# Quadrant tables for batches 0 and 1, and a new order, engines and banks for the opening of an attention and feed-forward kernel

## The chip, the cores and the metric

The kernel runs on one core of a Trainium2 chip. The metric is device time in microseconds (us). Three runs of the kernel before gave 321.02, 321.51 and 321.62 us, so its median is 321.51 us.

## What is computed

Eight batches of sliding-window attention with ALiBi slopes (8 heads, 576 tokens, 64 per head), and on its output a feed-forward layer with a hard swish. All inputs and the output are float32.

```python
def _attn_ref(q, k, v):                      # 8 x 8 x 576 x 64
    scores = scale * np.matmul(q, k.transpose(0, 1, 3, 2))
    slopes = 2.0 ** (-8.0 * (np.arange(H) + 1) / H)
    bias = slopes[:, None, None] * (-np.abs(rel))[None, :, :]   # rel = query - key
    mask = (rel >= 0) & (rel < 128)
    attn = softmax(np.where(mask, scores + bias[None], -1e9))
    return np.matmul(attn, v)
def _moe_ref(x, w_in, w_out):                # x 4608 x 512, w_in 512 x 2048
    h = x @ w_in
    return (h * np.clip(h + 3.0, 0.0, 6.0) / 6.0) @ w_out
```

## The kernel before, in words

**Attention.** A group g is one pair of heads of one batch: 8 batches of 4 pairs make 32 groups, g = 4 * batch + pair. A group's q and k are transposed to 64 x 576 for each head. Since the window is 128, each of the five key tiles of 128 needs two blocks of scores: the diagonal block, and the block with the next query tile. Both are made transposed (keys on partitions) in one of two score areas of PSUM, each of two banks, which take turns (`score_banks`). ScalarE takes the exponential into bf16 weights, `av_matmuls` multiplies them with v (with a column of ones, whose product is the sum), VectorE divides (`attend`, `attend_split`, `values`), and the result is transposed into xT (`back`), where the feed-forward layer reads it.

**Masks and slopes.** Where a group is *tabled*, a table of slope * (key - query), with -2^30 outside the window, is first written into the PSUM area by matmuls with the identity as weights, and the scores are added on top; the exponential then takes 1024 columns at once. In batch 0 both halves are tabled (`tables_diag`, `tables_off`), in batch 1 only the off half. Everything else takes slope and position through the exponential's bias, head by head, and GpSimd sets what is masked to zero (`affine_select`).

**Feed-forward.** xT's 4608 tokens are cut into 9 blocks of 512. A *unit* is four matmuls with 512 columns each: an up unit (`moe_up`, 16 for a block; ScalarE's relu and VectorE's product follow) or a quarter of a down product (`moe_down`, 16 for a block). A string, ORDER, gives the order of U and D; `fill(n)` runs the next n units, and FILLS gives the counts at seven places of each group.

**Order.** The program is scheduled by hand: every engine runs its instructions in the order of the code, and waits on semaphores. `first_batch` and `second_batch` write out the opening, groups 0 to 7 (batches 0 and 1, all tabled in part); `segment` then runs groups 8 to 31 with their fills. Transfers are issued from the queues of SP (q, k, v, the first quarter of w_in as float32), ScalarE (the first k) and GpSimd (the other weights, cast on the way). Where weights are not loaded yet, their room is used: batch 0's exponentials lie in w_out_sb, batch 1's in gbuf 1. Line numbers are those of the kernel before: L163 warm-up matmuls, L238 and L269/L281/L301 transposes of q and k, L321 and L357/L360 tables, L346 and L372/L378 scores of the opening, L399 scores after it, L422/L409 exponentials, L144 tables' making, L484/L485 division, L517 transposes of the result, L532 up and L587 down matmuls.

Of the kernel before, what the change touches and what calls it, by code (L numbers as in the profile page):

```python
# [18 lines left out]
def kernel(  # L19
# [29 lines left out]
    NB_FULL = 2  # L49
# [9 lines left out]
    tab = perm.tile([128, H, 2, 128], BF16)  # L59
# [20 lines left out]
    p4buf = [held.tile([128, 2, 128], BF16, name=f"p4buf{i}") for i in range(2)]  # L80
# [42 lines left out]

    def constants():
# [5 lines left out]
        base = rpool.tile([128, NT], FP32, tag="r6", name="base")  # L130
        base_i = base[:, 0:256].bitcast(INT32).rearrange("p (s c) -> p s c", s=2)
        base_b = base[:, 256:384].bitcast(BF16).rearrange("p (s c) -> p s c", s=2)
        nc.gpsimd.iota(base_i, pattern=[[128, 2], [0, 128]], base=-192, channel_multiplier=1)
        nc.gpsimd.tensor_copy(out=base_b, in_=base_i)
        biases()
        nc.gpsimd.affine_select(out=base_b[:, 1, :], in_=base_b[:, 1, :], pattern=[[1, 128]],
                                channel_multiplier=-1, base=0,
                                compare_op=ALU.is_ge, fill=-(2.0 ** 30))
        nc.gpsimd.affine_select(out=base_b[:, 0, :], in_=base_b[:, 0, :], pattern=[[-1, 128]],
                                channel_multiplier=1, base=-1,  # L140
                                compare_op=ALU.is_ge, fill=-(2.0 ** 30))
        nc.vector.memset(kTb[0][:, :, 4, LAST:128], 0.0)
        for h in range(H):
            nc.vector.tensor_scalar(out=tab[:, h, :, :], in0=base_b, scalar1=slopes[h] / scale,  # L144
                                    scalar2=0.0, op0=ALU.mult, op1=ALU.add)

    def memsets():
        nc.gpsimd.memset(vbuf[0][:, :, :, D:W], 1.0)
        nc.gpsimd.memset(vbuf[0][64:128, 4, :, 0:D], 0.0)

    def memsets_later():
        for i in range(2):
            nc.gpsimd.memset(p4buf[i], 1.0)
        nc.gpsimd.memset(kTb[1][:, :, 4, LAST:128], 0.0)
        nc.gpsimd.memset(vbuf[1][:, :, :, D:W], 1.0)
        nc.gpsimd.memset(vbuf[1][64:128, 4, :, 0:D], 0.0)
        nc.gpsimd.memset(tbuf[64:128, :, 4, :], 0.0)
# [7 lines left out]
    def biases():  # L165
        nc.vector.tensor_copy(out=rel_f, in_=rel_i)
        for h in range(H):
            nc.vector.tensor_scalar(out=bias_o[:, h:h + 1], in0=rel_f, scalar1=-192.0,
                                    scalar2=slopes[h], op0=ALU.add, op1=ALU.mult)

        for h in range(H):
            nc.vector.tensor_scalar(out=bias_d[:, h:h + 1], in0=rel_f, scalar1=-64.0,
                                    scalar2=slopes[h], op0=ALU.add, op1=ALU.mult)
# [20 lines left out]
    def second_w_in():  # L194
        nc.gpsimd.memset(w_out_sb[:, 4, 0:1], 0.0)
        load_w_in(1)
# [24 lines left out]
    st = {}  # L221

    def prepare(g, copies):
        for nm, copy in zip("qk", copies):
            pr = prs.tile([128, RT * D], BF16, tag=f"pr{nm}", name="pr",
                          padded_shape=[128, 2 * RT * D])
            copy(out=pr, in_=runs[nm][:, g % NP, :])
            st[g, nm] = pr

    def transposes(g, copies):  # L230
        b, hp = divmod(g, NP)
        for nm, dst, copy in (("q", qTb[b % 2], copies[0]), ("k", kTb[b % 2], copies[1])):
            src = st.pop((g, nm))
            tp = ps_h.tile([128, RT, RP], BF16, tag="h", name="tp", padded_shape=[128, 16, 64])
            for t in range(RT):
# [74 lines left out]
    def full(g):  # L310
        return g < NB_FULL * NP

# [574 lines left out]
```

## Time and profile before

| | us |
|---|---|
| median of three runs | 321.51 |
| the profiled execution: span from its first to its last instruction | 317.9 |
| TensorE busy in it | 307.0 |
| ScalarE busy | 196.8 |
| VectorE busy | 176.1 |
| GpSimd busy | 138.9 |
| opening: start of group 8's scores (L399) | 49.66 |
| start of group 9's scores | 59.97 |
| start of group 14's scores | 96.04 |

In the profile PE is TensorE, PEld its weight loads, DVE VectorE, ACT ScalarE, POOL GpSimd, SP the engine that only issues transfers. A row of the timeline has the start in us, the time taken, engine, line, operation, output and inputs, shapes, and how many instructions are merged; in brackets the idle time of the engine before it and what ended it. Matmuls overlap one another in the array, so the time between two starts says more than a duration.

### The profile page before, as it was taken

The numbers are of one execution on the slowest core, as the hardware profiler recorded it, in microseconds if no ns is written. First come the engines' busy times: TensorE is split into PE (matmuls) and PEld (weight loads), VectorE is DVE, ScalarE is ACT, GpSimd is POOL, SyncE is SP. The second block draws the span as 40 slices with busy tenths as digits, with TensorE's granted clock in tenths as the row PEclk, the third lists the DMA queues.
The fourth block names the chain that finished last, engine by engine and source line by source line (L and its number), as shares of the span: only waits on it lengthen the run. The fifth ranks groups of instructions, "written<-read, shape, count | busy, mean of one in ns | idle before, by whom it ended". The sixth has DMA issues, their size and how long they took to land.

```text
span 317.9 us, 6980 instructions
## 1 busy us (share of the span) xinstructions
PE 307.0 (97%) x2671; PEld 163.4 (51%) x2710; DVE 176.1 (55%) x344; ACT 196.8 (62%) x338; POOL 138.9 (44%) x247
## 2 busy tenths in 40 slices
PE   8889999999999999999999999999999999999996
PEld 3565474455554445555676644454444444444443
DVE  6677676554456654566465546564656455455510
ACT  3869986877767666766667756675764244244401
POOL 7358192674594684548463854472231000000000
PEclk9999999999999999999999999999999999999999
DMA  7999999999999999999999999934112100000112
GB/s 271 264 373 215 255 236 200 236 235 198 216 265 180 222 215 212 213 196 253 186 178 219 190 206 198 228 95 57 49 29 75 66 34 33 35 33 33 66 57 77
DMA packets 131425, 52.43 MB, mean 165 GB/s; under 512 B 118976, under 2 KB 122816, under 8 KB 131392
## 3 DMA queue, kind: packets, MB, share of 16 engines
q1 hardware_dynamic: 125648, 46.15, 69.0%
q0 software_dynamic: 3696, 3.67, 7.1%
q10 hardware_dynamic: 2048, 2.16, 2.2%
q8 instruction: 21, 0.34, 0.5%
q14 instruction: 12, 0.10, 0.1%
HBM read 36.70 MB, written 9.44 MB: 145 GB/s over the span
## 4 chain that ended last, share of the span: by engine, by line
PE 90%; ACT 3%; DVE 3%; issue 2%; POOL 0%; DVEq 0%; POOLq 0%; ACTq 0%
PE hps L532 38%; PE ops L587 37%; PE score L399 3%; PE av L463 2%; PE av L455 2%; DVE avs L485 1%; PE ops L568 1%; PE w L163 1%; ACT w_out_sb L422 1%; PE score L346 1%; PE tp L269 1%; ACT r L556 1%; DVE gbuf L557 1%; PE score L301 1%; PE score L357 1%
## 5 line engine op out<-in xcount | busy, mean ns | idle before, releaser
L556 ACT ACTIVATE r<-hps,bias 128x512 f32<-128x512 f32 x144 | 98.9, 689 | 84.2 <-PE hps L532 83.9
L557 DVE SCALAR_TENSOR_TENSOR gbuf<-r,hps 128x512 bf16<-128x512 f32 x144 | 98.8, 688 | 91.6 <-ACT r L556 90.1
L532 PE MATMUL hps<-xT,w_in_sb 128*128 128x512 bf16 (+1 forms) x623 | 142.0, 358 | 1.7 <-ACT xT L519 0.3
L587 PE MATMUL ops<-w_out_sb,gbuf 128*128 128x512 bf16 x538 | 133.8, 379 | 2.3 <-issue 1.8
L532 PEld LDWEIGHTS <-w_in_sb 128*128 128x128 bf16 x640 | 59.2, 98 | 54.0 <-issue 1.5
L587 PEld LDWEIGHTS <-gbuf 128*128 128x128 bf16 x560 | 52.4, 98 | 57.5
L427 POOL TENSOR_SCALAR_AFFINE_SELECT pd<-pd 128x512 bf16<-128x512 bf16 x48 | 29.4, 631 | 35.2 <-ACT pd L425 35.2
L436 POOL TENSOR_SCALAR_AFFINE_SELECT po<-po 128x512 bf16<-128x512 bf16 x48 | 30.1, 633 | 30.8 <-ACT po L434 30.1
L596 DVE COPY osb<-ops 128x512 f32<-128x512 f32 x33 | 22.7, 688 | 23.8 <-PE ops L587 23.7
L425 ACT ACTIVATE pd<-score,bias_d 128x512 bf16<-128x512 f32 x48 | 31.1, 683 | 6.4 <-PE score L399 6.4
L434 ACT ACTIVATE po<-score,bias_o 128x512 bf16<-128x512 f32 x48 | 33.1, 690 | 0.0
L213 POOL CAST tbuf<-ldbuf 128x512 bf16<-128x512 f32 (+1 forms) x45 | 25.7, 611 | 15.7 <-issue 14.6
L474 DVE TENSOR_TENSOR avs<-av,rc 128x384 bf16<-128x384 f32 (+1 forms) x48 | 23.6, 491 | 1.6
L463 PEld LDWEIGHTS <-pd 128*128 128x128 bf16 x192 | 14.3, 97 | 8.2 <-issue 0.2
L455 PE MATMUL av<-vbuf,po 128*128 128x65 bf16 x192 | 18.0, 193 | 0.0
L206 POOL CAST vbuf<-ldbuf 128x1024 bf16<-128x1024 f32 x14 | 14.3, 1041 | 7.6 <-DMA ldbuf<-in_v_dram 7.6
L463 PE MATMUL av<-vbuf,pd 128*128 128x65 bf16 x192 | 17.3, 194 | 0.0
L455 PEld LDWEIGHTS <-po 128*128 128x128 bf16 x192 | 14.3, 98 | 3.0 <-DVE avs L474 0.5
L439 ACT ACTIVATE p4buf<-score,bias_d 128x64 bf16<-128x64 f32 x48 | 15.6, 324 | 0.0
L399 PEld LDWEIGHTS <-kTb 64*64 64x64 bf16 x480 | 9.4, 106 | 9.1 <-issue 8.5
L399 PE MATMUL score<-qTb,kTb 64*64 64x192 bf16 (+1 forms) x480 | 13.1, 234 | 0.0
L246 POOL CAST pr<-ldbuf 128x576 bf16<-128x576 f32 x18 | 11.5, 668 | 2.6 <-PE tp L238 1.3
(107 smaller groups left out, 201.7 us busy)
## 6 DMA issues: line engine op xcount, KB each, us to landing
out_dram<-osb SPq DMA_DIRECT2D x33, 256.0 KB, 3.5
ldbuf<-in_v_dram SPq DMA_DIRECT2D x31, 256.0 KB, 4.6
ldbuf<-in_q_dram SPq DMA_DIRECT2D x20, 256.0 KB, 5.0
ldbuf<-in_k_dram SPq DMA_DIRECT2D x16, 256.0 KB, 5.3
ldbuf<-in_q_dram SPq DMA_DIRECT2D x12, 288.0 KB, 6.6
ldbuf<-in_k_dram SPq DMA_DIRECT2D x12, 288.0 KB, 6.7
w_out_sb<-in_moe_w_out_dram POOLq DMA_DIRECT2D x4, 512.0 KB, 9.1
w_in_sb<-in_moe_w_in_dram POOLq DMA_DIRECT2D x3, 512.0 KB, 8.8
```

Source lines behind the costliest of these rows:

```text
L213: nc.gpsimd.tensor_copy(out=tbuf[:m, :, j, :], in_=s[:m, j, :, :].rearrange("p (i e) d -> p i (e d)", e=2))
L399: nc.tensor.matmul(wide[e][c, ds(at, n)], lhsT=kT[r, j, c], rhs=qT[r, ds(q0, n)], start=True, stop=True)
L425: nc.scalar.activation(out=pd[:, e, :, :], in_=block_scores(g, e, False), func=ACT.Exp, bias=bias_d[:, h:h + 1], scale=scale)
L427: nc.gpsimd.affine_select(out=pd[:, e, :, :], in_=pd[:, e, :, :], pattern=[[0, 4], [1, 128]], channel_multiplier=-1, base=0, compare_op=AL ...
L434: nc.scalar.activation(out=po[:, e, :, :], in_=sc, func=ACT.Exp, bias=bias_o[:, h:h + 1], scale=scale)
L436: nc.gpsimd.affine_select(out=po[:, e, :, :], in_=po[:, e, :, :], pattern=[[0, 4], [-1, 128]], channel_multiplier=1, base=-1, compare_op=A ...
L455: nc.tensor.matmul(out_av, lhsT=po[:, e, (qt if full(g) else qt - 1) % 4, :], rhs=vb[:, qt - 1, h, :], start=True, stop=False)
L463: nc.tensor.matmul(out_av, lhsT=d, rhs=vb[:, qt, h, :], start=(qt == 0), stop=True)
L532: nc.tensor.matmul(hps[:, lo:hi], lhsT=w_in_sb[:, ks, ts(ms, 128)], rhs=xT[:, ks, ds(src, hi - lo)], start=(ks == 0), stop=(ks == n_ks - 1))
L556: nc.scalar.activation(out=r6, in_=hps, func=ACT.Relu, bias=bias3[:, 0:1], scale=1.0 / 6.0)
L557: nc.vector.scalar_tensor_tensor(out=gts[nt][:, ms, :], in0=r6, scalar=1.0, in1=hps, op0=ALU.min, op1=ALU.mult)
L587: nc.tensor.matmul(ops[nt, sub], lhsT=gts[nt][:, ms, ts(sub, 128)], rhs=w_out_sb[:, ms, :], start=(ms == 0), stop=(ms == n_ms - 1))
```

## The change

**Tables.** All groups of batches 0 and 1 are tabled in both halves, and the halves are cut otherwise: half 0 holds key tiles 0 and 1, half 1 holds key tiles 2, 3 and the short tile 4. The array is used in quadrants of 64 x 64, as L399 does it already: each head e reads its 64 rows, and each 64 keys c go to their own 64 partitions. The table's values are made as three rows of blocks (`base`), and one VectorE operation of 768 columns for each pair multiplies them with two slopes (`slope_table`; a column of slopes, one for each half of the partitions), instead of eight of 256.

**Order.** `first_batch` and `second_batch` become one list, `opening`, in which casts, copies, transposes, tables, scores, exponentials, values and units are placed one by one with the engine (V VectorE, P GpSimd, A ScalarE) and the PSUM bank (h, av, o) of each; the values of groups 1 and 5 are made in two parts in those banks (`attend_part`), the others in a score area. The divided values lie in tbuf. Warm-up matmuls are 4 and 3 instead of 5 and 3. The bias columns are made later, the order of U and D gets one string from start to end, and the FILLS of groups 8 to 13 change. `p4buf` has four buffers instead of two.

```diff
-    def tables_diag(g):
-        scd = score_banks()
-        st[g, "scd"] = scd
-        for e in range(2 if diag_tabled(g) else 0):
-            t = tab[:, 2 * (g % NP) + e, 1:2, :]
-            nc.tensor.matmul(scd[:, e, :].rearrange("p (j c) -> p j c", j=4), lhsT=ident,
-                             rhs=t.to_broadcast([128, 4, 128]), start=True, stop=False)
+    def tables(g, t):
+        hp = g % NP
+        sc = st[g, "sc", t] = score_banks()
+        for c in range(2):
+            o = slice(c * 64, (c + 1) * 64)
+            for e in range(2):
+                r = slice(e * D, (e + 1) * D)
+                src = tab[r, ds(hp * 768 + (c + 1 - e) * 256, 384)]
+                row = sc[o, e, :].rearrange("p (j c) -> p j c", j=2)
+                if t == 0:
+                    nc.tensor.matmul(row, lhsT=ident[r, r],
+                                     rhs=src[:, 0:256].rearrange("p (j c) -> p j c", j=1)
+                                     .to_broadcast([64, 2, 256]), start=True, stop=False)
+                    continue
+                nc.tensor.matmul(row[:, :, 0:192], lhsT=ident[r, r],
+                                 rhs=src[:, 0:192].rearrange("p (j c) -> p j c", j=1)
+                                 .to_broadcast([64, 2, 192]), start=True, stop=False)
+                nc.tensor.matmul(row[:, :, 192:256], lhsT=ident[r, r],
+                                 rhs=src.rearrange("p (s c) -> p s c", s=2)[:, :, 0:64],
+                                 start=False, stop=False)
...
+    def scores_full(g, t):
...
+        for j in (2 * t, 2 * t + 1):
+            for c in range(2):
+                q0 = j * 128 + c * 64
+                n = min(192, S - q0)
+                for e in range(2):
+                    r = slice(e * D, (e + 1) * D)
+                    nc.tensor.matmul(sc[ds(c * 64, 64), e, ds((j + t) % 2 * 256 + c * 64, n)],
+                                     lhsT=kT[r, j, ds(c * 64, 64)], rhs=qT[r, ds(q0, n)],
+                                     start=False, stop=(j % 2 == 1 and (t == 0 or c == 1)))
...
+    def exp_full(g, t):
+        at = 1024 * (1 - t)
+        nc.scalar.activation(out=room(g)[:, ds(at, 1024)], in_=st[g, "sc", t].rearrange(
+            "p e c -> p (e c)"), func=ACT.Exp, scale=scale)
...
-    def first_batch():
-        prepare(0, (V, A))
...
-        warm_up(5)
-        tables_diag(0)
-        tables_off(0)
-        transposes(0, (V, A))
-        warm_up(3)
-        scores_diag(0)
...
+    def opening():
+        slope_table(1)
+        nc.gpsimd.memset(p4buf[3], 1.0)
+        warm_up(4)
+        prep(0, "q", P)
+        kt_pad(1, nc.vector)
+        load_double(0, 1, "q", nc.sync)
+        slope_table(2)
+        load_double(0, 1, "k", nc.scalar)
+        slope_table(0)
...
+        tables(0, 0)
...
+        tables(0, 1)
+        prep(0, "k", V)
+        run_back(0, "q", "av", V)
+        run_back(0, "k", "h", V)
+        scores_full(0, 1)
+        prep(1, "q", A)
+        scores_full(0, 0)
+        run_back(1, "q", "o", A)
...
+        exp_full(0, 0)
+        warm_up(3)
...
     FILLS = {g: (1, 1, 1, 2, 0, 1, 1) for g in range(9, 15)}
     FILLS.update({g: (1, 0, 1, 2, 1, 1, 2) for g in range(4 * NP, G, NP)})
+    FILLS.update({8: (0, 3, 2, 1, 1, 0, 1), 9: (1, 2, 0, 2, 1, 0, 1), 11: (1, 2, 1, 1, 0, 1, 1), 12: (1, 0, 1, 1, 3, 0, 1), 13: (1, 1, 2, 1, 1, 0, 1), 10: (2, 1, 3, 0, 0, 0, 1)})
```

What stands on TensorE at group 0's tables, the end of its first table half and the start of the other, before:

```order
L321 LDWEIGHTS ident
L321 MATMUL score_115<-tab,ident 128x512
L357 LDWEIGHTS ident
L357 MATMUL score_114<-tab,ident 128x384
L360 LDWEIGHTS ident
L360 MATMUL score_114<-tab,ident 128x128
```

and the same place in the changed kernel, with the last quadrant of half 0 and the first and second of half 1:

```order
L322 LDWEIGHTS ident
L322 MATMUL score_118<-tab,ident 64x512
L326 LDWEIGHTS ident
L326 MATMUL score_117<-tab,ident 64x2x192
L329 LDWEIGHTS ident
L329 MATMUL score_117<-tab,ident 64x2x64
L326 LDWEIGHTS ident
L326 MATMUL score_117<-tab,ident 64x2x192
```

The full array's 384 and 128 columns become 2 x 192 and 2 x 64 in each of four quadrants, one quadrant after the other.

On VectorE at the start (ldbuf 100/101 here are q's and k's first loads, tp a transposed bank), before:

```order
L172 TENSOR_SCALAR bias_d<-rel_f 128x1 x8
L142 MEMSET kTb_112 128x4x32
L144 TENSOR_SCALAR tab<-base 128x256 x8
L227 CAST pr<-ldbuf_100 128x576
L239 COPY qTb_110<-tp 128x576
L227 CAST pr<-ldbuf_101 128x576
```

and in the changed kernel (ldbuf_102 is k's):

```order
L148 MEMSET tab 128x64
L151 TENSOR_SCALAR tab<-base,slope_65 128x768
L157 MEMSET kTb_116 128x4x32
L151 TENSOR_SCALAR tab<-base,slope_65 128x768 x2
L635 MEMSET p4buf_109 128x256
L227 CAST pr<-ldbuf_102 128x576
L239 COPY qTb_113<-tp 128x576
L239 COPY kTb_115<-tp 128x576
```

Three of the four pairs' tables, pair 0's as the third, stand ahead of the first cast, which is now k's; and both of pair 0's copies are on this engine.

On ScalarE from its first cast on, before:

```order
L227 CAST pr<-ldbuf_101 128x576
L117 DMA ldbuf_102<-in_v_dram 128x8x64
L239 COPY kTb_112<-tp 128x576
L422 ACTIVATE w_out_sb<-score_115 128x1024
L409 ACTIVATE w_out_sb<-score_114 128x1024
```

and in the changed kernel:

```order
L118 DMA ldbuf_103<-in_v_dram 128x8x64
L227 CAST pr<-ldbuf_101 128x576
L239 COPY qTb_113<-tp 128x576
L357 ACTIVATE w_out_sb<-score_118 128x1024
L357 ACTIVATE w_out_sb<-score_117 128x1024
L245 CAST pr_281<-ldbuf_102 128x9x64
L357 ACTIVATE w_out_sb<-score_118 128x1024
L285 COPY kTb_115<-tp_347 128x64x4
```

The copy ahead of the first exponential is now that of pair 1's q, and a cast of k stands between batch 0's second and third exponential.

More of the change, by code (lines that the diff above doesn't have):

```diff
@@ L129, in constants @@
         nc.gpsimd.iota(rel_i, pattern=[[0, 1]], base=0, channel_multiplier=1)
[L130 to L137, printed above, removed]
+        nc.gpsimd.iota(first_i, pattern=[[64, 3], [-128, 2]], base=-128, channel_multiplier=1)
@@ L141, in constants @@
                                 compare_op=ALU.is_ge, fill=-(2.0 ** 30))
[L142 to L157, printed above, removed]
+        nc.vector.memset(tab[:, NP * 768:], 0.0)
@@ L722, in first_batch @@
[L722 to L764 removed]
+        prep_half(1, 1, "k", 0, V)
```

590 lines of the change are left out of this document (306 added, 284 removed).

## The prediction

> **What bounds the kernel now.** I read the page's first lines, then the stretches of the span, then the engines' timelines of the first 60 us. The page's span and its chain:
>
> ```profile
> span 317.9 us, 6980 instructions
> PE 90%; ACT 3%; DVE 3%; issue 2%; POOL 0%; DVEq 0%; POOLq 0%; ACTq 0%
> ```
>
> TensorE carries 90% of the chain. The stretches (TensorE, weight loads, VectorE, ScalarE, GpSimd, clock, DMA):
>
> ```profile
> 8.00:17.50 9.50, 8.30 (x154) 5.22 (x153) 5.97 (x13) 8.58 (x10) 3.17 (x5) 1.00 1.22 284
> 17.50:23.40 5.90, 5.25 (x96) 4.26 (x97) 5.22 (x11) 3.52 (x6) 4.18 (x8) 1.00 1.07 378
> 23.40:49.70 26.30, 25.47 (x286) 14.64 (x292) 19.80 (x32) 23.76 (x36) 17.82 (x28) 1.00 1.14 232
> 60.00:96.00 36.00, 35.05 (x347) 18.61 (x351) 18.27 (x38) 26.96 (x50) 25.81 (x45) 1.00 1.11 231
> ```
>
> From 8 to 17.5 us ScalarE sets the pace (8.58 of 9.5), from 17.5 to 23.4 VectorE (5.22 of 5.9), from 23.4 on TensorE, with ScalarE close behind (23.76 of 26.3). The change touches the opening and the groups up to 13 only. So what it can win is the idle time of TensorE up to 96 us, and matmul work that it removes. The profiled execution's 317.9 us of span and some 3.6 us around it make the median of 321.5; I add my terms to that.
>
> **Prices on TensorE.** A matmul's duration in the trace holds its pipeline, so I take start to start. The diagonal half of a batch 1 group, its other half with tables, the scores of a later group, and units of the up and down products (L532, L587):
>
> ```profile
> 34.37 0.40 PE L346 MATMUL score<-qTb,kTb 64*128 64x128 bf16 x8
> 34.70 1.04 PE L532 MATMUL hps<-xT,w_in_sb 128*128 128x512 bf16 x4
> 35.57 0.33 PE L357 MATMUL score<-tab,ident 128*128 128x384 bf16 x1
> 35.74 0.22 PE L360 MATMUL score<-tab,ident 128*128 128x128 bf16 x1
> 35.79 0.33 PE L357 MATMUL score<-tab,ident 128*128 128x384 bf16 x1
> 35.95 0.22 PE L360 MATMUL score<-tab,ident 128*128 128x128 bf16 x1
> 36.44 1.90 PE L532 MATMUL hps<-xT,w_in_sb 128*128 128x512 bf16 x8
> 49.66 0.55 PE L399 MATMUL score<-qTb,kTb 64*64 64x192 bf16 x20
> 50.14 1.04 PE L587 MATMUL ops<-w_out_sb,gbuf 128*128 128x512 bf16 x4
> 51.01 1.03 PE L532 MATMUL hps<-xT,w_in_sb 128*128 128x512 bf16 x4
> ```
>
> A unit of four matmuls is 0.87 (50.14 to 51.01). A batch 1 group's diagonal half is 0.33 (34.37 to 34.70), its other half with tables 0.87 (35.57 to 36.44): 1.20 together. L399 puts 20 quadrant matmuls, 3200 columns, into 0.48; one after another they would be 1.34 at the unit's rate, so nearly four run at once.
>
> **Tables and scores of a group, new.** Half 0: four quadrants of 512 columns, which can run together as L399's do: 0.22, and eight scores in two rounds, 0.19, with the change of tile 0.50. Half 1 is the disputed price. Its tables are, for each quadrant, 384 columns and then 128 columns *into the same quadrant*, before the next quadrant's 384. In the rows above, the 128 starts 0.17 after the 384 before it, and the next 384 only 0.05 after that: starts keep the program's order. If they do so here, a quadrant's 128 waits for its 384, and the next quadrant's 384 waits behind that 128: four times 0.165 and a last 0.055, 0.71, and 0.25 for ten scores: 0.96. Bounds: 0.50, if the four quadrants' pieces overlap, and 1.13, if no piece overlaps at all. I take 0.96, being nearest to how the quoted rows start. A batch 1 group then costs 1.46, not 1.20: **+1.0 us for the four** (bounds -0.8 and +1.7). It lies in the stretch where TensorE is full, so it counts whole. The Trainium skill, page "TensorE: Matmul & The Clock Gate", Part 3, says that matmuls start and end in program order without reordering; by that, half 1 is 0.96 and the quadrants of half 1 don't run four at a time. No run here shows a table in quadrants yet.
>
> **The start.** Here are TensorE's first tables, transposes and second warm-up, then VectorE's and ScalarE's rows:
>
> ```profile
> 3.53 1.06 PE L321 MATMUL score<-tab,ident 128*128 128x512 bf16 x2
> 4.39 0.53 PE L357 MATMUL score<-tab,ident 128*128 128x384 bf16 x1
> 5.38 1.17 PE L238 MATMUL tp<-ident,pr 64*64 64x64 bf16 x36
> 6.48 1.16 PE L163 MATMUL w<-ident 128*128 128x512 bf16 x3
> 7.57 0.40 PE L346 MATMUL score<-qTb,kTb 64*128 64x128 bf16 x8
> 1.68 0.58 DVE L168 TENSOR_SCALAR bias_o<-rel_f 128x1 f32<-128x1 f32 x8
> 2.86 1.76 DVE L144 TENSOR_SCALAR tab<-base 128x256 bf16<-128x256 bf16 x8
> 8.41 0.76 DVE L239 COPY qTb<-tp 128x576 bf16<-128x576 bf16 x1 [0.93 <-PE tp L238]
> 9.08 0.75 DVE L239 COPY kTb<-tp 128x576 bf16<-128x576 bf16 x1
> 4.72 0.66 ACT L227 CAST pr<-ldbuf 128x576 bf16<-128x576 f32 x1
> 6.59 0.64 ACT L239 COPY kTb<-tp 128x576 bf16<-128x576 bf16 x1 [1.22 <-PE tp L238]
> 8.01 1.02 ACT L422 ACTIVATE w_out_sb<-score 128x1024 bf16<-128x1024 f32 x1 [0.78 <-PE score L346]
> 15.52 1.02 ACT L422 ACTIVATE w_out_sb<-score 128x1024 bf16<-128x1024 f32 x1
> 16.44 1.02 ACT L409 ACTIVATE w_out_sb<-score 128x1024 bf16<-128x1024 f32 x1
> ```
>
> TensorE first runs at half rate: two matmuls of 512 take 0.86 (3.53 to 4.39), and three at 6.48 still 1.09. The table of a head costs VectorE 0.22 for 256 columns, of which 0.07 is fixed (eight one-column operations in 0.58), so 768 columns are 0.48. The change makes the pairs' tables in the order 1, 2, 0, and pair 0's are the ones that TensorE wants first: from 2.86, three tables and a pad give 4.5, and TensorE's tables begin at 4.7, not 3.5. At half rate half 0 is 0.43 and half 1 1.4: 6.5. The 36 transposes of q and k follow (1.0): 7.5. Both are now copied by VectorE (0.67 apart, as at 8.41 and 9.08; before, ScalarE took k): 8.5. Then 18 scores and 18 transposes of pair 1 (0.8), and ScalarE copies those (0.64) *before* its first exponential, since that copy stands ahead in its queue: first exponential at 10.1, against 8.01. One wait is new and hidden: ScalarE holds the second half of a k transfer until the first load has landed, and the cast of pair 1's q is queued behind it; a load had landed when the cast at 4.72 began, so that cast is done by 7, and its transposes come after 8.5.
>
> Behind it stand eight exponentials 0.92 apart, as at 15.52 and 16.44 (7.4), a cast of k (0.66, as at 4.72) and a copy of 256 columns (less than the 0.64 of 576 at 6.59; I take 0.45). The two score areas take turns: while ScalarE reads one (0.93), TensorE must refill the other, and half 1 with its 0.96 and the signals is late by some 0.25, three times. So batch 0's exponentials end near 19.4, where the row at 16.44 ends at 17.46. DMA is not the cause: its order and bytes up to the raw weights are nearly the same.
>
> The values follow. VectorE takes about 1.04 for each of four (17.43 to 21.60):
>
> ```profile
> 16.16 0.43 DVE L200 CAST vbuf<-ldbuf 128x512 bf16<-128x512 f32 x1 [1.53 <-DMA ldbuf<-in_v_dram]
> 17.43 0.22 DVE L484 RECIPROCAL rcw<-score 128x10 f32<-128x10 f32 x1 [0.84 <-PE score L463]
> 20.78 0.82 DVE L485 TENSOR_TENSOR avs<-score,rcw 128x640 bf16<-128x640 f32 x1
> 22.68 0.45 DVE L519 COPY xT<-tb 128x576 bf16<-128x576 bf16 x1
> 21.81 0.44 PE L517 MATMUL tb<-ident,avs 128*128 128x128 bf16 x5
> 22.86 0.66 PE L301 MATMUL score<-ident,pr 128*128 128x128 bf16 x9 [0.18 <-ACT pr L256]
> 26.68 0.66 PE L301 MATMUL score<-ident,pr 128*128 128x128 bf16 x9 [0.23 <-ACT gbuf L425]
> ```
>
> In the new order the first part of pair 1 stands behind the last scores in TensorE's queue (18.3), VectorE begins at 18.75, and it has the four values in five pieces (4.0), a transposed copy (0.45, as at 22.68) and a weight cast (0.43, the shape at 16.16) ahead of the last: 4.9, so 23.65. The transposes of pair 3, at 21.81 before, come at 23.7: 1.9 later. TensorE has then one up matmul more behind it (0.2), and doesn't stand idle as it did before the row at 22.86 (22.09 to 22.86 but for one matmul, 0.55). **Net +1.1**, of which I take +1.0. Bounds: if the tables overlap and the clock is up, 0.5 a group and 1.4 at the start are gone, and the last v, cast at 16.16 to 16.6, holds the values: -0.3; at half rate all the way, +2.5.
>
> **What it saves.** Two exponentials of 512 and one of 1024 become two of 1024 in batch 1, and eight masks on GpSimd go. ScalarE and GpSimd get lighter, but TensorE hides both. What counts are TensorE's waits that this and the new banks remove: 0.4 ahead of the row at 26.68, and part of 0.6 between 49.66 and the next scores:
>
> ```profile
> 59.97 0.55 PE L399 MATMUL score<-qTb,kTb 64*64 64x192 bf16 x20
> 98.26 0.23 PE L463 MATMUL av<-vbuf,pd 128*128 128x65 bf16 x2
> 98.56 1.89 PE L532 MATMUL hps<-xT,w_in_sb 128*128 128x512 bf16 x8
> ```
>
> Ten units (8.7), a set of scores (0.48) and 9 transposes (0.5) are 9.7 of that 10.3. **I take -0.8** (0 to -1.5). The rest of the matmul work up to group 9's scores is the same 28 units. After that, up to group 14, the new lists of fills place 32 units where 31 stood. Before, 31 units (27.0), five scores (2.4), five groups of values (ten matmuls in 0.30, so 0.54 each), transposes (1.8) fill 33.9 of 36.0, so there is room for it: **-0.5** (0 to -0.9). The smaller edits (slope memsets, biases later, pads, four p4 buffers, the avs in tbuf) lie on VectorE and GpSimd beside a full TensorE; if that cover went, the sixteen bias columns would be 1.2.
>
> **Sum.** +1.0 (start) +1.0 (batch 1's tables) -0.8 -0.5 = +0.7: 317.9 + 0.7 + 3.6 = **322.2**.
>
> **Rivals.** *The quadrants' pieces overlap after all.* Then batch 1 is -0.8, the start about -0.1, and with -0.8 and -0.5 the sum is -2.2: 319.3. For it: L399's 0.48. Against: its neighbours are always different quadrants. *In order, but well fed:* the start loses only 0.5, since the walk above adds every signal in one line, and the waits give all 1.5 and 0.9: +0.5 +1.0 -2.4 = -0.9, 320.6. For it: the batch 1 units take turns on four banks, not two; against: the start's queue order. *The clock stays at half:* slower. Five warm-ups become four, and TensorE then stands from 3.1 to 4.7 for the table of pair 0; before, it ran from 1.43 and the rate rose only after 6.5. If the rise waits until about 11, each group's refill of 0.5 + 0.96 nearly doubles for one to two groups: +1.5, 323.7. It decides if 512 columns still take over 0.4 after 8 us. The Trainium skill, the same page, Part 1, says that a busy window of about 3.4 us lifts the clock; with it this rival holds only if the pause breaks that window, and the rows at 6.48 agree that 5 us from the first matmul weren't enough.
>
> **Chances.** Forecast 0.50 (0.30 of it above +0.2%, 0.20 within), overlapping 0.25, well fed 0.12, half clock 0.13. Differences under 0.2% (0.64 us) a measurement of this kernel can hardly tell from none. So faster 0.37, same 0.20, slower 0.43. The signs are mixed: the forecast's own range is 321.2 to 323.4, and the one for 8 in 10 goes from within the overlapping case, 318.8, into the half clock, 323.9.
>
> **What would show it.** In the changed profile: the first exponential near 10 and batch 0's last ending near 19.4; four quadrant pairs of half 1 starting 0.22 apart in steps of 0.17 and 0.05, not within 0.02; pair 3's transposes near 23.7; scores of group 8 near 51 to 53 with 20 units done, of group 9 near 61 (59.97 before). A first exponential before 9, half 1 tables within 0.3, or group 9 before 59 make the prediction wrong.

## The result and the profile after

The changed kernel took **323.59 us** (median of 6 runs, 323.22 to 324.95), the kernel before 320.75 (6 runs, 319.76 to 321.62, the first three runs among them): a ratio of **1.0096, 95% interval 1.0070 to 1.0122**. The ratio is an estimate from the single fast runs, so it isn't quite the quotient of the medians, 1.0089. The forecast was 322.2, in a range of 318.8 to 323.9. The time is in the range, near its slow end; most of the steps were not what I had said. The page of the changed kernel, its span and its chain:

```profile
span 321.5 us, 7093 instructions
PE 82%; DMA 7%; issue 4%; DVE 3%; POOL 2%; ACT 2%; SPq 0%; POOLq 0%
```

TensorE had 90% of the chain and DMA none; now DMA has 7%. Before the parts, the milestones of both profiled executions:

| us | before | after |
|---|---|---|
| first exponential starts | 8.01 | 9.60 |
| batch 0's last exponential ends | 17.46 | 20.40 |
| transposes of pair 3's values | 21.81 | 25.00 |
| scores of group 8 (units done) | 49.66 (18) | 53.59 (20) |
| scores of group 9 (units done) | 59.97 (28) | 63.89 (28) |
| scores of group 14 | 96.04 | 99.72, one unit ahead |
| scores of group 17 | 119.28 | 123.72, one unit ahead |
| span | 317.9 | 321.5 |

With 0.87 for a unit: +2.2 up to group 8 (3.93 less two units), +1.7 from there to group 9 (the units are level again), -1.1 to group 14, +0.8 from 14 to 17, nothing after: +3.6, the difference of the spans. The medians differ by 2.8 only, since the profiled execution before was a short one. Now where each comes from. Timeline rows of TensorE in the opening:

```profile
8.95 1.46 PE L167 MATMUL w<-ident 128*128 128x512 bf16 x3
12.36 1.68 PE L279 MATMUL tp<-ident,pr 128*128 128x128 bf16 x14
...
16.78 0.37 PE L326 MATMUL score<-tab,ident 64*64 64x384 bf16 x4 [0.37 <-ACT w_out_sb L357]
...
25.79 1.03 PE L506 MATMUL hps<-xT,w_in_sb 128*128 128x512 bf16 x4
```

Three matmuls of 512 columns take 1.39 from start to start (8.95 to 10.34), 0.46 each: still half rate at 9, where the kernel before was at full rate after 7. Fourteen transposes at 12.36 take 1.60. Only at 16.8 is the rate full (384 columns take 0.37; at 13.96 still 0.55). The last row is the first whole unit; before, it started 2.43 earlier, with three up matmuls done ahead of it in both kernels:

```profile
23.36 1.03 PE L532 MATMUL hps<-xT,w_in_sb 128*128 128x512 bf16 x4
```

Next, a batch 1 group of the changed kernel; half 0 begins at 36.26, half 1 at 38.59, and each ends where the next unit starts:

```profile
36.26 0.41 PE L322 MATMUL score<-tab,ident 64*64 64x512 bf16 x4
36.50 0.33 PE L346 MATMUL score<-qTb,kTb 64*64 64x192 bf16 x8
36.76 1.90 PE L506 MATMUL hps<-xT,w_in_sb 128*128 128x512 bf16 x8
38.59 0.37 PE L326 MATMUL score<-tab,ident 64*64 64x384 bf16 x4
38.78 0.24 PE L329 MATMUL score<-tab,ident 64*64 64x128 bf16 x4
38.84 0.33 PE L346 MATMUL score<-qTb,kTb 64*64 64x192 bf16 x8
39.00 0.20 PE L352 MATMUL score<-qTb,kTb 64*64 64x64 bf16 x2
39.13 1.04 PE L506 MATMUL hps<-xT,w_in_sb 128*128 128x512 bf16 x4
```

Half 0 is 0.50, as forecast. Half 1 is **0.54, not 0.96**: all four quadrants' 384 columns go at once (one merged row, and the records of the group at 27.26 have them within 0.02 of each other), then all four 128s, 0.19 later. The program gives a 384 and a 128 to one quadrant after another; the starts don't keep that order. A group is 1.04 against 1.20 before, so batch 1 *saves* 0.6. Then the new waits of TensorE and what GpSimd's queue did meanwhile:

```profile
48.67 0.68 PE L295 MATMUL score<-ident,pr 128*128 128x128 bf16 x9 [0.54 <-POOL pr L245]
57.76 1.02 PE L558 MATMUL ops<-w_out_sb,gbuf 128*128 128x512 bf16 x4 [1.18 <-DMA w_out_sb<-in_moe_w_out_dram]
61.21 1.02 PE L558 MATMUL ops<-w_out_sb,gbuf 128*128 128x512 bf16 x4 [0.70 <-DMA w_out_sb<-in_moe_w_out_dram]
```

```profile
38.60 0.74 POOL L191 DMA_DIRECT2D w_out_sb<-in_moe_w_out_dram  x1
...
42.69 0.74 POOL L191 DMA_DIRECT2D w_out_sb<-in_moe_w_out_dram  x1
47.33 1.89 POOL L245 CAST pr<-ldbuf 128x576 bf16<-128x576 f32 x3 [3.90 <-DMA ldbuf<-in_q_dram]
49.16 1.48 POOL L191 DMA_DIRECT2D w_out_sb<-in_moe_w_out_dram  x2
```

GpSimd stands 3.90 us for batch 2's q, and behind those casts in its queue stand the last two loads of w_out. Before, they were given out at 45.13 and 45.89 and landed at 54.06 and 57.52; now at 49.16 and 49.89, landing at 57.71 and 61.16, each just before the row that waited. And q is late for two reasons: it was given out at 38.09 to 39.99 instead of 34.01 to 39.51, and the first w_out load, at 38.60, went ahead of three of its four loads (e5 tests this). q landed at 43.57, 45.87, 47.21 and 48.61; before, all was in by 45.13.

### The profile page after: what moved, and what is told of

Same layout as the page of the kernel before. It is cut to its first block, busy times and chain, and to the rows that moved or that the text cites. A ratio compares the mean times of both kernels' runs of the same rounds, so it can differ in the third digit from the quotient of the medians.

```text
span 321.5 us, 7093 instructions
## 1 busy us (share of the span) xinstructions
PE 309.4 (96%) x2765; PEld 164.0 (51%) x2765; DVE 178.6 (56%) x361; ACT 195.5 (61%) x334; POOL 130.1 (40%) x233
## 4 chain that ended last, share of the span: by engine, by line
PE 82%; DMA 7%; issue 4%; DVE 3%; POOL 2%; ACT 2%; SPq 0%; POOLq 0%
PE ops L558 37%; PE hps L506 33%; DMA w_out_sb<-in_moe_w_out_dram 4%; PE score L380 3%; DMA ldbuf<-in_q_dram 2%; PE av L432 2%; PE av L430 2%; DMA ldbuf<-in_k_dram 1%; PE ops L539 1%; ACT w_out_sb L357 1%; POOL pr L245 1%; PE tp L279 1%; PE tp L268 1%; PE score L346 1%; PE tp L237 1%
## 5 line engine op out<-in xcount | busy, mean ns | idle before, releaser
L506 PE MATMUL hps<-xT,w_in_sb 128*128 128x512 bf16 (+1 forms) x640 | 143.7, 358 | 0.7 <-DVE gbuf L528 0.4
L558 PE MATMUL ops<-w_out_sb,gbuf 128*128 128x512 bf16 x560 | 137.8, 379 | 1.9 <-DMA w_out_sb<-in_moe_w_out_dram 1.9
L390 ACT ACTIVATE pd<-score,bias_d 128x512 bf16<-128x512 f32 x48 | 31.8, 683 | 9.1 <-PE score L380 9.1
L399 ACT ACTIVATE po<-score,bias_o 128x512 bf16<-128x512 f32 x48 | 33.1, 689 | 0.0
L206 POOL CAST vbuf<-ldbuf 128x1024 bf16<-128x1024 f32 x12 | 12.1, 1040 | 0.0
L245 POOL CAST pr<-ldbuf 128x576 bf16<-128x576 f32 x12 | 7.9, 668 | 9.0 <-DMA ldbuf<-in_q_dram 6.0
```

Source lines behind the costliest of these rows:

```text
L390: nc.scalar.activation(out=pd[:, e, :, :], in_=block_scores(g, e, False), func=ACT.Exp, bias=bias_d[:, h:h + 1], scale=scale)
L399: nc.scalar.activation(out=po[:, e, :, :], in_=sc, func=ACT.Exp, bias=bias_o[:, h:h + 1], scale=scale)
L506: nc.tensor.matmul(hps[:, lo:hi], lhsT=w_in_sb[:, ks, ts(ms, 128)], rhs=xT[:, ks, ds(src, hi - lo)], start=(ks == 0), stop=(ks == n_ks - 1))
L558: nc.tensor.matmul(ops[nt, sub], lhsT=gts[nt][:, ms, ts(sub, 128)], rhs=w_out_sb[:, ms, :], start=(ms == 0), stop=(ms == n_ms - 1))
```

## The experiments

**Theory:** what the change loses are waits for loads, passed on by queues that run in order. **Rivals:** the cold start; the tables; the order of the units. Times in us are medians of 4 to 12 runs; the ratio, with its interval, is to runs of the kernel before that were made together with them. The runs were made on several chips, so rows are compared by their ratios. The other columns are the start of a group's scores and the span, in one profiled execution each.

| run | us | ratio | group 8 | 9 | 14 | 16 | span |
|---|---|---|---|---|---|---|---|
| the change | 323.59 | 1.0096 (1.0070 to 1.0122) | 53.59 | 63.89 | 99.72 | 115.13 | 321.5 |
| e1_warm | 324.64 | 1.0152 (1.0125 to 1.0179) | 53.44 | 63.56 | 99.39 | 114.80 | 321.2 |
| e2_wout | 323.29 | 1.0113 (1.0058 to 1.0167) | 54.72 | 62.82 | 100.45 | 115.94 | 322.3 |
| e3_tail | 323.44 | 1.0101 (1.0067 to 1.0134) | 57.44 | 65.53 | 101.37 | 116.57 | 322.4 |
| e5_w0 | 322.48 | 1.0073 (1.0052 to 1.0095) | 52.89 | 62.33 | 98.15 | 114.22 | 320.6 |
| e6_loads | 322.82 | 1.0077 (1.0039 to 1.0116) | 53.84 | 63.02 | 98.86 | 114.45 | 320.8 |
| e7_all | 322.30 | 1.0053 (1.0022 to 1.0085) | 55.79 | 63.78 | 99.61 | 114.81 | 320.6 |
| e8_early | 323.09 | 1.0081 (1.0056 to 1.0106) | 54.56 | 63.88 | 99.71 | 115.41 | 321.4 |
| e9_qcast | 323.03 | 1.0086 (1.0061 to 1.0111) | 52.38 | 64.44 | 100.27 | 115.68 | 322.0 |
| e10_best | 346.27 | 1.0799 (1.0761 to 1.0836) | 79.48 | 87.47 | 123.30 | 138.63 | 344.5 |
| e11_best2 | 322.20 | 1.0053 (1.0025 to 1.0082) | 53.24 | 61.23 | 97.07 | 114.13 | 320.0 |
| e12_best3 | 323.06 | 1.0075 (1.0047 to 1.0103) | 51.51 | 60.10 | 97.35 | 117.21 | 323.0 |

Executions of one program vary, so these columns need care. Up to group 13 e3 is the changed kernel, yet its group 8 comes at 57.44 instead of 53.59. The profiled execution of e1 is the shortest of its four (spans of 321.2 to 323.7), that of e12 the longest of its nine (319.6 to 323.0). A difference in a column is put down to an edit below only where a row shows the wait that went or came.

**The clock at the start (e1_warm).**

```diff
-        warm_up(4)
+        warm_up(6)
...
         run_back(0, "q", "av", V)
+        warm_up(1, "o")
         run_back(0, "k", "h", V)
+        warm_up(2, "o")
```

> The changed kernel with six warm-up multiplies instead of four ahead of the first tables, one more (into the bank of the next transposes) between the transposes of q and k of pair 0, and two more ahead of the first scores, so that TensorE has no pause over 0.3 us between 1.4 and 8. Theory (the clock): in the changed kernel four pauses of 0.34 to 0.86 us kept TensorE at half rate until about 16 us (14 transposes from 12.36 took 1.61), and without them it is at full rate by about 8, as before the change. Then the 14 transposes take about 0.8, batch 0's last exponential ends near 19.4 instead of 20.40 and pair 3's transposes come near 24.0 instead of 25.00; the span falls by 0.5 to 1.0 from 321.5. Rival (the chain of copies and casts): the start waits for VectorE, ScalarE and the second k load, the clock is beside the path; the last exponential ends within 0.3 of 20.40 and the span stays within 0.3. Rival (the pauses have nothing to do with the clock): the 14 transposes still take about 1.6.

Timeline rows of TensorE in this run:

```profile
8.43 0.82 PE L167 MATMUL w<-ident 128*128 128x512 bf16 x3
12.09 1.11 PE L279 MATMUL tp<-ident,pr 128*128 128x128 bf16 x14
23.62 0.45 PE L491 MATMUL tb<-ident,tbuf 128*128 128x128 bf16 x5
48.51 0.68 PE L295 MATMUL score<-ident,pr 128*128 128x128 bf16 x9 [1.74 <-POOL pr L245]
```

Three matmuls of 512 now end within 0.82, at full rate, and pair 3's transposes come at 23.62 instead of 25.00. So the pauses of 0.34 to 0.86 did hold the clock down. But the 1.4 us won at 24 are a longer wait at 48.51 (1.74 instead of 0.54, for the same casts of batch 2), and group 8 comes 0.15 earlier. The clock theory is right, and beside the point: loads set group 8. The time isn't shorter either: the ratio, 1.0152, is the highest of the single edits, and why it lies above that of the change is open.

**w_out earlier (e2_wout).**

```diff
         load_w_out(1)
+        load_w_out(2)
+        load_w_out(3)
...
-        load_w_out(2)
...
-        load_w_out(3)
```

> The changed kernel with the third and fourth loads of w_out given out by GpSimd right behind the second (near 43.4 and 44.2 instead of 49.16 and 49.89), ahead of the casts of batch 2's q. Theory (late w_out): the two waits of 1.18 and 0.70 at 57.76 and 61.21 vanish, the stage from the scores of group 8 to those of group 9 takes 8.2 to 8.7 instead of 10.30, and the span falls by 1.5 to 2.2 to 319.3 to 320.0. Rival (the transfers compete): the earlier w_out holds up batch 2's q, the casts that ended its wait at 47.33 come 1 to 2 later, the scores of group 8 come as much later than 53.59, and the span stays within 0.5 of 321.5.

Stage 8 to 9 takes 8.10 instead of 10.30: the waits for w_out are gone, as the theory said. Group 8 came 1.13 later, which the rival had; but q didn't take longer (its last load 8.79 from issue to landing, 8.62 in the changed kernel), it was given out 0.8 later. The span didn't fall. The wait moved to the next loads; TensorE's row in group 10, and GpSimd's:

```profile
72.77 0.45 PE L268 MATMUL tp<-ident,pr 128*128 128x128 bf16 x5 [1.73 <-POOL pr L253]
```

```profile
71.25 1.47 POOL L253 CAST pr<-ldbuf 128x576 bf16<-128x576 f32 x2 [5.25 <-DMA ldbuf<-in_k_dram]
```

Batch 3's k, for which GpSimd waited 2.68 in the changed kernel and TensorE not at all, landed behind w_out and v and q blocks.

**The unit order (e3_tail) and the tables' order (e4_tab).** The first sets back 16 letters of ORDER; the second gives out all four 384s of half 1 and then all four 128s.

```diff
-...UDUUUDDUDDUDDUUU...
+...UDUDUDUUDUDUDDUU...
```

> The changed kernel with 16 letters of the unit order (units 64 to 79, in groups 13 to 17) set back to those of the kernel before: UDUDUDUU DUDUDDUU instead of UDUUUDDU DDUDDUUU. Theory (three U units in a row): the two waits of TensorE for VectorE's product (0.39 in the row at 120.17 and the like near 108) go, the stage from the scores of group 14 to those of group 17 takes 23.2 to 23.4 instead of 24.0, and the span falls by 0.5 to 0.8. Rival (the stage is long for another cause, the groups' own order of work): the stage stays within 0.2 of 24.0 and the span with it.

> The changed kernel with the second half's table multiplies in another program order: first the 384 columns of all four quadrants, then the 128 columns of all four, instead of 384 and 128 of one quadrant after another. Theory (quadrants overlap whatever the order): the four 384s already start within 0.02 of each other in the trace of the changed kernel, so nothing moves, 128s 0.16 behind the 384s, span within 0.3 of 321.5. Rival (the order counts, as the prediction had it): each second half gets 0.35 shorter and the time falls by up to 1.0 where TensorE is the bound, in batch 1.

e3: groups 14 to 17 take 23.24 (101.37 to 124.61), as before the change, instead of 24.00: the order of units costs 0.76. Its span is no shorter since this execution lost more ahead of group 8, where the edit doesn't reach, and the time of its four runs isn't shorter either (ratio 1.0101); its rows and its stretches of 2 us (TensorE's clock is the third number from the end):

```profile
48.96 1.53 PE L506 MATMUL hps<-xT,w_in_sb 128*128 128x512 bf16 x4 [3.36 <-ACT xT L493]
```

```profile
48.00:50.00 2.00, 1.04 (x4) 0.48 (x4) 0.00 (x0) 2.00 (x4) 0.60 (x1) 0.83 1.14 283
50.00:52.00 2.00, 2.00 (x19) 1.73 (x18) 1.15 (x2) 0.73 (x2) 2.00 (x5) 0.50 1.20 203
52.00:54.00 2.00, 2.00 (x19) 1.52 (x18) 1.05 (x2) 0.00 (x0) 0.70 (x1) 0.81 1.28 266
```

ScalarE's copy for pair 0 of batch 1 stood in its queue behind casts of batch 2's late halves; TensorE paused 3.36 us and then ran at half clock for some 3.4 us, which costs 1.7 more. e4 took 323.68 (ratio 1.0102, 1.0070 to 1.0133), no different. Its profiled execution waited 3.99 where e3's waited 3.36, so only its table rows are compared:

```profile
31.09 0.36 PE L326 MATMUL score<-tab,ident 64*64 64x384 bf16 x4
31.28 0.23 PE L335 MATMUL score<-tab,ident 64*64 64x128 bf16 x4
31.33 0.33 PE L352 MATMUL score<-qTb,kTb 64*64 64x192 bf16 x8
```

0.19 and 0.05, as in the changed kernel: the order in which the quadrants' pieces are given out changes nothing.

**The order of the loads (e5_w0, e6_loads).** e5 moves `load_w_out(0)` behind a cast of batch 2's k. e6 does more:

```diff
-        load_w_out(0)
...
-        hold(2, 0, nc.gpsimd)
...
         prep_half(2, 1, "k", 1, P)
+        load_w_out(0)
+        load_w_out(1)
...
         prep_half(2, 0, "k", 0, P)
+        load_w_out(2)
+        load_w_out(3)
+        hold(2, 0, nc.gpsimd)
+        load_block(2, "v", 3, nc.sync)
...
         load_double(3, 0, "k", nc.sync)
+        load_block(3, "q", 1, nc.sync)
+        load_block(3, "q", 2, nc.sync)
```

> The changed kernel with one line moved: the first load of w_out, 0.5 MB, is given out by GpSimd behind the cast of a half of batch 2's k (near 41.1) instead of ahead of it at 38.60, so behind the last of batch 2's q loads (issued 39.99) instead of ahead of three of them. Theory (transfers go about in the order of their issue, and w_out stands ahead of batch 2's q): q's loads land near 45.5 instead of 48.61, GpSimd's casts that began at 47.33 begin near 44.5, and the scores of group 8 come near 51 to 52 instead of 53.59; part of it is lost again to the later w_out loads, so the span falls by 0 to 2 from 321.5. Rival (the transfers share the queues evenly, so the order doesn't matter): q still lands within 1 of 48.6 and the casts stay at 47.

> The changed kernel with the order of the loads from 38 to 66 us put back about as it was before the change: w_out 0 and 1 behind batch 2's q and k, w_out 2 and 3 ahead of the casts of q, then v of batch 2, then k and q of batch 3; engines, banks, tables and unit order stay as changed. Theory (the order of the loads is what the change loses): q's loads land by 46, the scores of group 8 come at 50.5 to 52, no wait for w_out over 0.3 is left, stage 8 to 9 takes 8.1 to 8.6, and the span falls by 3 to 4.5 to 317.0 to 318.5, level with the kernel before or under it. Rival (the cost lies in the tables and the cold start, the loads are late only because everything is): the span falls by under 1.

In e5 q landed at 43.70, 44.41, 45.37 and 47.80, and GpSimd's casts began 1.8 earlier:

```profile
45.49 1.90 POOL L245 CAST pr<-ldbuf 128x576 bf16<-128x576 f32 x3 [1.76 <-DMA ldbuf<-in_q_dram]
```

The last q came only 0.81 earlier, where the theory said 3.1 and the rival allowed 1. All the runs together are clearer: with a w_out load ahead of it the last q load took 8.62 to 11.03 from issue to landing (six runs), with w_out behind it 5.46 to 8.19 (seven runs). So transfers do come about in the order of issue. Group 8 gains 0.7 only, group 9 1.6. e6 missed: group 8 at 53.84, and still 0.45 and 0.63 of waits for w_out, whose last part landed at 60.30. One reason is mine: the hold covers a column of v's block 0, while v's first load here is block 3, which went ahead of w_out and landed at 54.08. Its span fell by 0.7, which is what the rival said (under 1); the tables aren't the cost, though, since they save 0.6, and e7, which adds the mended start and the unit order, gains 0.2 more.

**Sums (e7_all, e8_early), and the cast order (e9_qcast).** e7 adds e1's and e3's edits to e6. e8 also puts `load_double(0, 1, ...)` ahead of the constants, as before the change. e9 is the changed kernel with `prep_half(2, 1, "q", 0, P)` three casts later.

> The load order of the run before this one, and with it the 16 letters of the unit order set back (stage 14 to 17: 23.24 instead of 24.0) and the five more warm-up multiplies (pair 3's transposes 1.4 earlier). Theory (once the loads no longer set it, the start counts): the span falls by 0.7 more for the unit order and by 0.5 to 1.2 more for the start, to 315.5 to 317.0, faster than the kernel before. Rival (DMA still sets group 8): the start adds nothing, only the 0.7 shows.

> As the run before this one, and the loads of pairs 2 and 3 (q and k) are given out ahead of the constants, as before the change, instead of behind them. Theory (the second k load, held on ScalarE's queue until 4.50, made its cast wait until 11.47): its cast comes 1.0 to 1.3 earlier, batch 0's last exponential and pair 3's transposes about 0.7 earlier than in the run before this one; the span falls by up to 0.7 more if the start counts by then, by nothing if DMA sets group 8. Rival: the four loads take the queues from the first two pairs, and the first exponential comes later than 9.6.

> The changed kernel with one line moved: GpSimd casts the first half of q of pairs 2 and 3 of batch 2, which is used in group 9 only, behind the halves of pairs 0 and 1 and of k instead of ahead of them. Theory (an order on GpSimd's queue that puts a late load first): the other two casts no longer wait for the load that landed at 47.21, so they come when their own load is in, near 45.9 to 46.5; the transposes of pairs 0 and 1 come 0.5 to 1.3 earlier than 48.67 and the scores of group 8 up to 1 earlier than 53.59, while the waits for w_out (1.18 and 0.70) stay; the span falls by 0.3 to 1.0. Rival (TensorE is dense up to there but for the 0.54 ahead of 48.67): at most 0.5 is won.

e7 missed: its span is 320.6, where 317.0 at most was said. e8 differs from e7 by the early loads alone, and they do little: ScalarE's cast comes at 10.73 instead of 11.12, pair 3's transposes at 22.49 instead of 22.35. Nor does the better start show at group 8: e7 waits 2.26 for w_out at 50.54, e8 1.88 for a copy at 45.64. e9 shows the trade best; timeline and stretches of TensorE:

```profile
57.49 1.02 PE L558 MATMUL ops<-w_out_sb,gbuf 128*128 128x512 bf16 x4 [2.12 <-DMA w_out_sb<-in_moe_w_out_dram]
58.35 3.34 PE L506 MATMUL hps<-xT,w_in_sb 128*128 128x512 bf16 x8
...
62.62 1.89 PE L506 MATMUL hps<-xT,w_in_sb 128*128 128x512 bf16 x8
```

```profile
58.00:60.00 2.00, 2.00 (x8) 0.77 (x7) 0.00 (x0) 0.00 (x0) 0.00 (x0) 0.66 1.11 215
60.00:62.00 2.00, 2.00 (x5) 0.70 (x5) 0.69 (x1) 0.96 (x2) 0.00 (x0) 0.50 0.47 107
```

Group 8 comes 1.2 earlier, so the wait for w_out is longer (2.12 instead of 1.18), the clock drops, eight up matmuls take 3.34 instead of 1.89, and group 9 is later than without the edit.

**TensorE's queue mended (e10_best, e11_best2, e12_best3).** Casts for batch 2 behind ScalarE's copies, w_out 0 to 3 behind batch 2's q, the load of v held, batch 3's k and q after it, the first D after more U, and e1's and e3's edits. The core of e12:

```diff
         back(5, "av", A)
+        unit("h")
+        prep_half(2, 0, "k", 1, A)
+        prep_half(2, 0, "q", 0, A)
...
+        wide_begin(2, 0, "k")
+        wide_begin(2, 0, "q")
+        wide_copy(2, 0, "k", 0, 2, A)
         unit("o")
+        wide_copy(2, 0, "q", 0, 2, V)
```

> The changed kernel with all that the runs so far point to: the five more warm-up multiplies; w_out 0 behind batch 2's q, and 1 to 3 ahead of the casts of q, a hold on v of batch 2 that holds its first block, then k and q of batch 3; the casts of batch 2's halves that ScalarE makes behind its copies for pairs 0 and 1 instead of ahead of them, and GpSimd's cast for group 9 last; the transposes of batch 2's pairs 0 and 1 behind two and three more units; the first unit of the second product behind three of the first; and the 16 letters of the unit order set back. Theory (what the change lost were waits of queues for loads, not tables): no wait of TensorE over 0.5 between 25 and 90, scores of group 8 at 50.5 to 52, group 9 8.0 to 8.4 later, group 14 to 17 23.2; span 315.5 to 317.5, so 0.1% to 0.8% under the kernel before. Rival (the loads come no earlier than they do, and TensorE waits for them wherever the casts stand): the scores of group 8 stay at 53 or later or a wait of over 1 moves on to group 10, and the span stays at 319 to 321.

> The run before with two things mended: the loads of batch 3's k stand behind ScalarE's casts of batch 2's halves again (they write to the room that those casts read, and made ScalarE wait 23.7), and the first four D units stand one place later each (units 20, 22, 25 and 28), since w_out 0 to 3 landed at 50.32, 53.66, 56.95 and 60.42. Theory (what the change lost were waits of queues for loads, not tables): no wait of TensorE over 0.6 between 25 and 90, scores of group 8 at 50.5 to 52, group 9 8.0 to 8.6 later, groups 14 to 17 23.2; span 315.5 to 317.8, 0.05% to 0.8% under the kernel before. Rival (batch 2's loads are late wherever the casts stand): the scores of group 8 at 53 or later, or a wait of over 1 at the transposes of batch 2 or of group 10; span 319 to 321.

> The run before with TensorE's two own waits mended: ScalarE's two casts of batch 2's halves stand behind the activation of the unit that they held up (TensorE waited 1.43 for its product at 46.72), and both transposes of batch 2 stand ahead of the last four units instead of one and two units later (the scores of group 8 waited 1.25 for a copy of q). Theory A (TensorE's queue alone): the scores of group 8 come at 50.5 to 51.2 instead of 53.24, all later stages 2.0 to 2.7 earlier, the span 317.3 to 318.0, no slower than the kernel before. Theory B (behind TensorE stands the stream of loads, which stays as late as it is: the transposes of batch 4's q by DMA landed at 99.97 before the change and at 103.08 in the run before this one, GpSimd's cast of batch 4's k waited for it, and the scores of group 16 came at 114.1 to 114.8 in five of the runs, whenever those of group 14 came): the scores of group 8 come earlier just so, but those of group 16 stay at 113.3 or later, with waits for GpSimd's masks ahead of them, and the span falls by under 1 to 319 or more.

In e10 ScalarE's cast stood behind batch 3's load into the room that it reads, so for one half it takes batch 3's k and leaves out batch 2's; the cast waited 23.7 and TensorE 25.26. It says only what one misplaced load costs. e11's group 8 (53.24) and span (320.0) are what its rival said, but for another reason: TensorE had no wait for a load up to group 8, but two of my own making:

```profile
46.72 1.02 PE L506 MATMUL hps<-xT,w_in_sb 128*128 128x512 bf16 x4 [1.43 <-DVE gbuf L528]
...
53.24 0.55 PE L380 MATMUL score<-qTb,kTb 64*64 64x192 bf16 x20 [1.25 <-DVE qTb L300]
```

e12 takes these away: group 8 at 51.51, the best of all, which is level with the kernel before (49.66 with two units less, so 51.4). And the span is 323.0. TensorE waits at 69.68 for a cast of batch 3's k, for which GpSimd had waited 3.79. Its rows there and in group 15, and GpSimd's:

```profile
69.68 0.45 PE L268 MATMUL tp<-ident,pr 128*128 128x128 bf16 x5 [1.36 <-POOL pr L253]
...
104.52 0.55 PE L380 MATMUL score<-qTb,kTb 64*64 64x192 bf16 x20
108.06 0.20 PE L432 MATMUL av<-vbuf,pd 128*128 128x65 bf16 x1 [1.15 <-POOL pd L392]
...
117.21 0.55 PE L380 MATMUL score<-qTb,kTb 64*64 64x192 bf16 x20
```

```profile
104.58 2.83 POOL L213 CAST tbuf<-ldbuf 128x512 bf16<-128x512 f32 x5 [6.96 <-issue]
107.37 1.21 POOL L392 TENSOR_SCALAR_AFFINE_SELECT pd<-pd 128x512 bf16<-128x512 bf16 x2
```

These are the signs of theory B, in one execution; the three of the nine whose mean granted clock was 1.00 had spans of 319.6 to 320.2. GpSimd waits 6.96 to cast batch 4's k into tbuf, which a transfer still reads (the row names no releaser, but the transfer lands 0.11 ahead of it): the transposes of batch 4's q landed at 104.47 (99.97 before the change, 102.07 in the changed kernel). The masks of group 14 stand behind that cast, TensorE waits for the masks, then runs at half clock (0.53 and 0.62 between 110 and 114), and stage 15 to 16 takes 12.69 instead of 8.03. Nor are the transfers at their limit there. The stretches from 84 to 92 us, e12 and then the kernel before (the last two numbers are DMA's share and GB/s):

```profile
84.00:88.00 4.00, 3.84 (x49) 2.25 (x48) 1.44 (x3) 2.81 (x6) 1.51 (x3) 1.00 0.74 174
88.00:92.00 4.00, 3.71 (x46) 2.03 (x46) 1.21 (x3) 1.47 (x4) 4.00 (x7) 1.00 0.75 168
```

```profile
84.00:88.00 4.00, 3.82 (x53) 2.09 (x51) 1.06 (x3) 3.38 (x7) 2.48 (x4) 1.00 1.18 238
88.00:92.00 4.00, 3.56 (x49) 2.06 (x47) 1.59 (x4) 2.22 (x4) 4.00 (x8) 1.00 1.11 301
```

The loads are late because they are given out late, on SP's queue, behind transposes (78.75 instead of 75.76) that wait for casts of loads that were late themselves. That last chain is read from the records and was not tested.

No version beat the kernel before. e7 and e11 give back nearly half of the loss (1.0053 against 1.0096), though their intervals still touch that of the change. Still open: why batch 2's first k is given out at 35.24 instead of 31.98 already in the changed kernel, and whether earlier loads for batches 3 to 5 would let the 0.6 of the tables show. No run puts the quadrant tables alone into the kernel before.

## Why the prediction was near in time and wrong in its steps

- **Batch 1's tables, +1.0: failed, in sign too.** Half 0 was right (0.50). Half 1 was taken as strictly in program order, 0.96; it took 0.54, so the term is -0.6. That was the first rival, to which I gave 0.25. The Trainium skill, page "TensorE: Matmul & The Clock Gate", Part 3, says that matmuls start in program order without reordering; the quadrants here (four 384s within 0.02, the 128s 0.19 later, in either program order) don't agree, and the measurement decides. The row to go by was L399's, which I quoted and set aside (I read it as nearly four at once; 3200 columns one after another are 1.36, against 0.48: 2.8 at once).
- **The start, +1.0: mis-sized, about +2.4** by the first whole unit; +2.3 is what the other terms leave of the 2.2 up to group 8 (plus the 0.6 of the tables, less the 0.5 of the wait). First exponential 9.60 (10.1 said), last one's end 20.40 (19.4), pair 3's transposes 25.00 (23.7). The half clock, a rival at 0.13, came true and was larger than the 1.5 that I gave: pair 3's transposes come at 24.44 to 25.34 in the seven runs without the added warm-up and at 22.31 to 23.62 in the six with it, 2.4 apart in the mean (21.81 before the change). e1, where a late k held ScalarE's cast for 0.99, is the latest of the six. So the half rate is most of the start's loss. But e1 and e7 also show that the start was covered: what it gives up, the loads take back at group 8.
- **"DMA is not the cause" and the waits removed, -0.8: the step that failed most.** I checked the transfers up to the raw weights and let the rest go; the bounds "0 to -1.5" held no new wait. The wait at the old row at 26.68 is gone (0.23 in the row; I took 0.4), but 0.54, 1.18 and 0.70 came, all for loads of 38 to 62 us. The order of GpSimd's queue, which was there to be read, has load_w_out 2 and 3 behind casts of batch 2's q, and load_w_out 0 ahead of its loads.
- **One more unit up to group 14, -0.5: right in kind, -1.1 in size**; but I took nothing from 14 on, and three U in a row gave 0.76 back (e3).

The terms as measured are +2.3 -0.6 +0.5 +1.7 -1.1 +0.8 = +3.6 in place of +0.7. That the time lay inside the range is luck, twice over. A tables term 1.6 too high stood by chance where the waits for w_out were missing. And the 3.6 that I put around the span is no cost of the program: in the runs on record the time is 1.66 to 2.85 above the span, mostly 1.7, so that 317.9 belonged to a faster execution than the 321.51 did. With 1.7 the same sum is 320.3 and the range ends at 322.0, below the measured 323.59. The slow end, 323.9, stood on the half clock alone, which was real, but e1 and e7 show that mending it alone doesn't give the time back.

## What to carry to other kernels

When a change reorders an opening, walk every queue that issues transfers (GpSimd's and SP's too) to the place where the last load of the opening lands, and write beside each load who waits for it and what stands ahead of it: a cast that waits for a late load holds up every load and mask behind it. Where loads follow one another closely, an edit that makes TensorE earlier can only lengthen its next wait, as in e1 and e9; so take away one wait, look where the next one is, and believe the gain only at the end of the span. Price small matmuls in quadrants by a row in which quadrants run, whatever the order in the program.

## What the runs showed of the hardware

- **Short pauses hold the clock down.** In the changed kernel TensorE ran at half rate until about 16 us, with pauses of 0.34 to 0.86 between 3.3 and 7.6; with these filled by five more matmuls (e1) it was at full rate at 8.43. The three warm-up matmuls take 0.82 in all six runs with the fill and 1.46 in all seven without. The column of the granted clock reads 1.00 there in both; only the durations show it.
- **A pause of about 2 us costs twice.** After pauses of 1.88 (e8), 2.12 (e9) and 3.36 (e3) the granted clock was 0.50 for some 3.4 us; after 1.74 (e1) and 1.73 (e2) it stayed at 1.00. One long pause isn't needed: in e12 it fell at 110 after four pauses of 1.15, 0.38, 0.38 and 0.35 within 3 us. The Trainium skill, page "TensorE: Matmul & The Clock Gate", Part 1, puts the way down at an idle window of about 3.4 us; here less was enough, while the time at half clock agrees with that window.
- **Pieces for different quadrants don't wait for each other's program order**: four 384s together, four 128s 0.19 behind, 0.25 for the tables of a half.
